# Block-sparse attention and gated MLP on one core: head 0's queries transposed in fp32, one mask product for two thirds, first attention products in slots 4 to 6

## The chip, the core and the metric

The kernel runs on one core of a Trainium2 chip. TensorE (PE) multiplies matrices into PSUM, VectorE (DVE), ScalarE (ACT) and GpSimd (POOL) do the elementwise work, and the queue of SyncE (SP) issues most of the DMAs; two DMAs are issued by ScalarE's queue. The metric is the time of one execution on the device in microseconds (us). A profiled execution gives the trace from which all lines here come: its instructions cover a span that is a little shorter than the execution's time.

## The reference

Inputs: `q`, `k`, `v` of shape (4, 8, 768, 64), fp32; three sampled key blocks for each of 24 query blocks; the weights of a gated MLP.

```python
scores = scale * np.matmul(q, k.transpose(0, 1, 3, 2))      # 4 x 8 heads, 768 x 768
mask = np.abs(blk_i - blk_j) <= 1                           # blocks of 32
mask = mask | (blk_i == 0) | (blk_j == 0) | (blk_i == 23) | (blk_j == 23)
# ... and for each query block its 3 sampled key blocks
attn = softmax(np.where(mask, scores, -1e9))
x = np.matmul(attn, v)  -> (4, 768, 512)
h = np.maximum(x @ w_in, 0.0); u, v = halves of h
v_s = einsum(w_spatial, layernorm(v)) + b_spatial
out = (u * v_s) @ w_out
```

The four batches need 32 heads of attention and four passes of the MLP.

## The kernel before, in words

**Data layout.** `kq` holds for each of 8 heads, on 128 partitions, the transposed keys (columns 0 to 767) and the transposed queries (columns 768 to 1535). Partitions 0 to 63 carry the head's 64 dimensions, partitions 64 to 127 the mask: one-hot block rows beside the keys, and for each query the penalty of each block beside the queries. One product of the two over 128 partitions is then score plus penalty, and the exponential makes masked entries zero. The mask rows are the same for all heads: they are made once for head 0 (`kq[MX, 0, ...]`, MX is partitions 64 to 127) and copied to the others by `rows`, partly on VectorE, partly on POOL, partly on ScalarE. The queries' mask rows are made by `mask_rows`: a product of `bm` (24 block rows) with the one-hot rows into PSUM, 256 columns (a third of the 768, TW) at a time, and a copy out of PSUM.

**Setup.** Keys and queries come as fp32 with 128 partitions of rows (`load`), are cast to bf16 (`cast`), transposed on TensorE against an identity (`head`, `tr`) and copied out of PSUM to `kq` (`split0` for pair 0, plain copies for the others). Pair 0 is heads 0 and 1, and head 0's parts come first: keys of chunks 0 to 3 on ScalarE's DMA queue, then queries of chunks 0 to 3 on the same queue, the rest on SP's. Head 0's keys are cast by ScalarE, its queries by POOL (`cast(0, "q", PL, H0, C03)`). In the cast the chunks are put in an order in which one transpose holds chunk i on its lower and chunk i + 2 on its upper 64 partitions, so `split0` copies chunks 0 and 1 from the lower half and 2 and 3 from the upper.

**Slots.** After the setup the work is dealt to slots, written out by hand. In slot s TensorE does the score products of one piece (`qk_unit`; from slot 36 on `qk_full`), into one of two PSUM buffers, and ScalarE takes their exponential. Since there are two buffers, the product of slot s waits for the exponential of slot s - 2. Units 0 and 1 are heads 0 and 1 of pair 0 with two thirds of the queries; each takes three slots. Slot 0 makes 4 small products in two PSUM tiles with an exponential for each; slot 2 makes the last two key chunks against 512 query columns. Behind the score product of a slot stand, on TensorE, in this order: what `pre` holds, the attention products (`av_unit`, three pieces of 8 products of 65 columns for a unit), what `at` holds, the MLP's steps (`run_queue`), what `late` holds. `av_at` says which attention piece stands in which slot: before, unit 0's three pieces stand in slots 5, 6 and 6.

Around the change: in slot 0 `second` transposes head 0's last two key chunks; in slot 1 `third` transposes head 1's keys and first queries (from POOL's casts of head 1); in slot 2 the third mask product follows; in slot 3 VectorE copies mask rows (`ROWS`); in slots 4, 7 and 9 the pairs 1, 2 and 3 are transposed (`tr_first`). POOL's stream after the setup is casts in the order of `ORDER`, as their loads land. Small products against `warm` (`filler`) keep TensorE at work in the setup: FILL at the start and FILL2 in three places.

**PSUM.** Four kinds of tile: two buffers "sc" for scores, two "av" for attention products, and "moeA" and "moeB", which `moe_tag` hands out in turn.

## Time and profile before

| | |
|---|---|
| median of 3 runs | 210.06 us (209.82 to 210.76) |
| profiled execution | 210.04 us |
| its span | 208.3 us |
| TensorE busy | 201.0 us (97%) |
| ScalarE busy | 168.4 us (81%) |
| VectorE busy | 146.8 us (70%) |
| POOL busy | 89.4 us (43%) |

A row of the timeline or of the chain gives the start and the length in us of one instruction or of several merged ones (x8), the engine, the line, the operation and the tiles as out<-in. In brackets stands the idle time of the engine ahead of it and what ended it. A row of the stage table gives a stretch, its length, then busy us and number of instructions for PE, PEld (the loading of weights), DVE, ACT and POOL, then the granted clock, the DMA engines' share and GB/s. Matmuls are pipelined: a length holds the way through the array, and the next one can start long before the end.

### The profile page before, as it was taken

How to read it: one execution, taken by the hardware profiler on the slowest of the kernel's cores; microseconds unless marked ns; L12 is line 12 of the kernel's file. 1: busy time of each engine (PE TensorE's matmuls, PEld its weight loads, DVE VectorE, ACT ScalarE, POOL GpSimd, SP SyncE). 2: the span in 40 equal slices, each digit the busy share in tenths (PEclk: the TensorE clock that was granted, in tenths of full speed). 3: DMA queues.
4: the chain of work that ended last, by engine and by line, in shares of the span. 5: the costliest groups of instructions: out<-in, count | busy, mean ns of one | idle time of the engine just before them, and what ended most of it. 6: DMA issues, size and time to landing. Idle time of an engine off the chain costs nothing.

```text
span 208.3 us, 5489 instructions
## 1 busy us (share of the span) xinstructions
PE 201.0 (97%) x2203; PEld 138.0 (66%) x2225; DVE 146.8 (70%) x315; ACT 168.4 (81%) x222; POOL 89.4 (43%) x186
## 2 busy tenths in 40 slices
PE   6899999999999999999999999999999999999993
PEld 6599888777766776667556676667665567445551
DVE  6888776989876766575975585456875666576871
ACT  6899999999999999989899878889899884266021
POOL 6888989767927964006757600006210000013000
PEclk9999999999999999999999999999999999999999
DMA  5999899999999999499987920499402010610016
GB/s 143 338 362 357 275 383 270 206 247 389 253 253 308 259 300 208 139 199 386 292 176 206 139 41 0 164 189 335 75 0 41 0 37 4 250 57 0 0 70 232
DMA packets 53053, 39.48 MB, mean 190 GB/s; under 512 B 33956, under 2 KB 47652, under 8 KB 53028
## 3 DMA queue, kind: packets, MB, share of 16 engines
q1 hardware_dynamic: 52596, 38.74, 70.0%
q10 hardware_dynamic: 432, 0.39, 0.6%
q8 instruction: 17, 0.28, 0.5%
q14 instruction: 8, 0.07, 0.1%
HBM read 24.77 MB, written 6.29 MB: 149 GB/s over the span
## 4 chain that ended last, share of the span: by engine, by line
PE 87%; DVE 4%; ACT 4%; DMA 2%; issue 1%; POOL 0%; ACTq 0%
PE ps L428 21%; PE ps_moe L630 17%; PE ps_moe L561 13%; PE ps_av L476 12%; PE ps L415 7%; PE ps_av L458 4%; PE ps_t L561 4%; PE ps_t L630 4%; PE ps_sc L630 2%; ACT a_all L420 2%; DVE stats L594 2%; DVE vn L185 2%; DMA st_q<-in_q_dram 2%; PE ps_sc L561 1%; PE ps L263 1%
## 5 line engine op out<-in xcount | busy, mean ns | idle before, releaser
L431 ACT ACTIVATE a_all<-ps 128x768 bf16<-128x768 f32 x144 | 113.4, 812 | 13.8 <-PE ps L428 6.2
L428 PE MATMUL ps<-kq 128*128 128x512 bf16 (+1 forms) x288 | 70.3, 326 | 0.3
L476 PEld LDWEIGHTS <-a_all 128*128 128x128 bf16 x864 | 46.6, 98 | 19.0
L476 PE MATMUL ps_av<-vv,a_all 128*128 128x65 bf16 x864 | 51.1, 194 | 0.1
L428 PEld LDWEIGHTS <-kq 128*128 128x128 bf16 x288 | 27.9, 97 | 23.6
L137 POOL CAST nat<-st_k 128x256 bf16<-128x256 f32 (+3 forms) x37 | 17.7, 509 | 38.7 <-DMA st_k<-in_k_dram 38.7
L420 ACT ACTIVATE a_all<-ps 128x1024 bf16<-128x1024 f32 x35 | 33.5, 1027 | 0.3
L630 PE MATMUL ps_moe<-w_spt,vn 128*128 128x512 bf16 (+1 forms) x144 | 33.1, 325 | 0.0
L598 POOL TENSOR_SCALAR std<-mv 128x3 f32<-128x3 f32 (+1 forms) x9 | 3.4, 376 | 48.7 <-DVE mv L595 48.5
L661 DVE TENSOR_TENSOR sb<-ps_moe,b_row 128x512 f32<-128x512 f32 x18 | 12.4, 690 | 14.5 <-PE ps_moe L630 14.2
L630 PE MATMUL ps_moe<-xt,w_in_t 128*128 128x256 bf16 (+1 forms) x108 | 21.7, 299 | 0.2
L415 PE MATMUL ps<-kq 128*128 128x256 bf16 x135 | 20.8, 275 | 0.8 <-DVE kq L211 0.6
L561 PE MATMUL ps_moe<-w_in_t,xt 128*128 128x512 bf16 x65 | 20.2, 378 | 0.2
L137 POOL CAST vv<-st_v 128x256 bf16<-128x256 f32 (+2 forms) x37 | 18.5, 533 | 3.9 <-DMA st_v<-in_v_dram 3.8
L137 POOL CAST nat<-st_q 128x256 bf16<-128x256 f32 (+2 forms) x41 | 19.2, 496 | 1.6 <-DMA st_q<-in_q_dram 1.5
L561 PE MATMUL ps_moe<-w_out_t,un 128*128 128x512 bf16 x64 | 19.4, 378 | 0.2
L441 DVE TENSOR_TENSOR xn<-ps_av,rc 128x384 bf16<-128x384 f32 (+1 forms) x36 | 18.5, 513 | 1.4 <-DVE rc L440 0.2
L664 DVE TENSOR_TENSOR un<-sb,un 128x512 bf16<-128x512 f32 x24 | 17.4, 727 | 1.5
L630 PEld LDWEIGHTS <-vn 128*128 128x128 bf16 x192 | 15.5, 97 | 4.4
L594 DVE BATCH_NORM_STATS2 stats<-vn 128x6 f32<-128x512 bf16 x24 | 16.5, 688 | 1.5 <-ACT vn L589 0.9
L211 DVE COPY osb<-ps_moe 128x512 f32<-128x512 f32 x12 | 8.3, 689 | 11.2 <-PE ps_moe L561 9.3
L211 DVE COPY kq<-tt 64x1536 bf16<-64x1536 bf16 x24 | 15.4, 641 | 0.6 <-DMA tt<-nat 0.2
(94 smaller groups left out, 241.6 us busy)
## 6 DMA issues: line engine op xcount, KB each, us to landing
out_dram<-osb SPq DMA_DIRECT2D x23, 256.0 KB, 2.1
st_k<-in_k_dram SPq DMA_DIRECT2D x15, 384.0 KB, 4.6
st_v<-in_v_dram SPq DMA_DIRECT2D x15, 384.0 KB, 6.2
st_q<-in_q_dram SPq DMA_DIRECT2D x12, 384.0 KB, 4.9
ws_f<-in_moe_w_spatial_dram SPq DMA_DIRECT2D x6, 384.0 KB, 5.5
w_f<-in_moe_w_in_dram SPq DMA_DIRECT2D x8, 256.0 KB, 6.3
w_f<-in_moe_w_out_dram SPq DMA_DIRECT2D x4, 256.0 KB, 5.4
st_q<-in_q_dram SPq DMA_DIRECT2D x3, 256.0 KB, 6.9
```

What stands on the lines that cost most here:

```text
L137: eng.tensor_copy(out=dst, in_=src)
L211: nc.vector.tensor_copy(out=o, in_=i)
L415: nc.tensor.matmul(out=ps[:, at:at + n * TW], lhsT=kq[:, h, ci * 128:(ci + 1) * 128], rhs=kq[:, h, qcols(t0, n)], start=True, stop=True)
L420: nc.scalar.activation(out=out, in_=ps, func=AF.Exp, scale=0.125)
L428: nc.tensor.matmul(out=ps[:, n0:n1], lhsT=kq[:, j % H, ci * 128:(ci + 1) * 128], rhs=kq[:, j % H, S + n0:S + n1], start=True, stop=True)
L431: nc.scalar.activation(out=a_ref["h", j][:, ci, :], in_=ps[:, 0:S], func=AF.Exp, scale=0.125)
L441: nc.vector.tensor_tensor(out=out, in0=ps[:, :, 0:D], in1=rc[:, 0:n].to_broadcast([128, n, D]), op=ALU.mult)
L476: nc.tensor.matmul(out=av_ref[j][:, qc, :], lhsT=a_ref["h", j][:, ci, qc * 128:(qc + 1) * 128], rhs=vv[p % NVV][:, h, ci, :], start=(ci == ...
L561: nc.tensor.matmul(out=ref["ps"][:, 0:w], lhsT=lhs(i), rhs=rhs(i), start=(i == 0), stop=(i == n - 1))
L594: nc.vector.bn_stats(out=stats, in_=self.vn[:, tcc, :])
L630: nc.tensor.matmul(out=o.rearrange("p (c t) -> p c t", c=n), lhsT=lhs(i)[:, (d0 + x) * 128:(d0 + x + 1) * 128], rhs=rhs(i), start=(i == 0) ...
L664: nc.vector.tensor_tensor(out=self.in_place(*area), in0=sb, in1=self.in_place(*area), op=ALU.mult)
```

## The change

1. `ident_f`, an fp32 copy of the identity, is made by POOL. A memset of part of `kq` goes, since no mask product reads it any more.
2. POOL's cast of head 0's queries goes. Four fp32 transposes read the loaded queries as they are: chunks 0 and 1, then 2 and 3, each once into `psq` and once into `psr`, two PSUM tiles of fp32. `q_part` copies 64x128 pieces: the lower halves from `psq` by VectorE, the upper halves from `psr` by ScalarE. The cast to bf16 happens in these copies.
3. One mask product over 512 columns (two thirds) takes the place of two over 256; it reads only the 24 mask partitions. Its copy out is on ScalarE, 512 wide.
4. Row copies of the keys' mask: head 2's goes whole to POOL (before: 512 columns on ScalarE and 256 on POOL), queued ahead of head 1's query cast. Head 5's moves from VectorE's setup to slot 3.
5. Fillers: 2 and 6 in place of 2, 2 and 2.
6. Unit 0's attention pieces stand in slots 4, 5 and 6. The one in slot 4 stands at the slot's end, after pair 1's transposes.

```diff
-    FILL, FILL2 = 26, (2, 2, 2)
+    FILL, FILL2 = 26, (2, 6)
...
+    ident_f = const.tile([128, 128], FP32)
...
-    nc.gpsimd.memset(kq[0:D, 1, 0:TW], 0.0)
+    nc.gpsimd.tensor_copy(out=ident_f, in_=ident)
...
-    cast(0, "q", PL, H0, C03)
     cast(0, "k", PL, H0, C45)
     cast(0, "k", PL, H1)
+    rows(slice(2, 3), K_, PL)
     cast(0, "q", PL, H1, C03)
...
-    def mask_rows(ps, t, copy, h=0, rs=slice(0, KR)):
-        nc.tensor.matmul(out=ps[:, 0:TW], lhsT=bm[rs], rhs=kq[rs, h, t * TW:(t + 1) * TW],
+    def mask_rows(ps, t, copy, h=0, rs=slice(0, KR), n=1):
+        nc.tensor.matmul(out=ps[:, 0:n * TW], lhsT=bm[rs], rhs=kq[rs, h, t * TW:(t + n) * TW],
                          start=True, stop=True)
-        copy(kq[MX, 0, qcols(t)], ps[0:MX.stop - MX.start, 0:TW])
+        copy(kq[MX, 0, qcols(t, n)], ps[0:MX.stop - MX.start, 0:n * TW])
...
     filler(FILL2[0], wps)
-    mask_rows(psum.tile([128, 1024], FP32, tag="sc", bufs=2, name="mq"), 0, act_copy, 1)
-    rows(slice(2, 3), slice(0, 512), nc.scalar)
+    mask_rows(psum.tile([128, 1024], FP32, tag="sc", bufs=2, name="mq"), 0, act_copy, 1, MR, 2)
+    psq = [psum.tile([128, 512], FP32, tag="av", bufs=2, name="psq"),
+           psum.tile([128, 512], FP32, tag=moe_tag(), bufs=1, name="psr")]
+    for i in range(TC):
+        for ps in psq:
+            nc.tensor.transpose(out=ps[:, i * 128:(i + 1) * 128],
+                                in_=st["q", 0][:, 0, 2 * i * D:2 * (i + 1) * D], identity=ident_f)
+
+    def q_part(i, odd, copy):
+        copy(kq[0:D, 0, S + (2 * i + odd) * 128:S + (2 * i + odd + 1) * 128],
+             psq[odd][odd * D:(odd + 1) * D, i * 128:(i + 1) * 128])
+
+    q_part(0, 0, dve_copy)
+    q_part(0, 1, act_copy)
+    split0(ps0, 0, *K4, 1)
     filler(FILL2[1], wps)
-    psq = bank("psq", "av")
-    head(psq, 0, *Q4)
-    split0(psq, 0, *Q4, 0)
-    split0(ps0, 0, *K4, 1)
-    filler(FILL2[2], wps)
-    mask_rows(psum.tile([128, 512], FP32, tag=moe_tag(), bufs=1, name="mq"), 1, act_copy, rs=MR)
-    split0(psq, 0, *Q4, 1)
-    rows(slice(4, 6), K_)
+    q_part(1, 0, dve_copy)
+    q_part(1, 1, act_copy)
+    rows(slice(4, 5), K_)
     rows(H1, qcols(0, 2), PL)
-    rows(slice(2, 3), slice(512, S), PL)
...
-    ROWS = [(3, 2, 8, qcols(0)), (5, 6, 8, K_),
+    ROWS = [(3, 2, 8, qcols(0)), (3, 5, 6, K_), (5, 6, 8, K_),
...
-            sl = (5, 6, 6)[e] if u == 0 else 3 * u + e + (4 if u < 3 else 3)
+            sl = (4, 5, 6)[e] if u == 0 else 3 * u + e + (4 if u < 3 else 3)
...
-        for u, e in av_at.get(s, []):
-            av_unit(u, e)
+        if s > 4:
+            for u, e in av_at.get(s, []):
+                av_unit(u, e)
...
         for f in late.get(s, []):
             f()
+        if s == 4:
+            av_unit(0, 0)
```

## The prediction

> **What bounds the kernel now.** I read the page's chain of waits first, to learn which engine carries the span, then the stage table, then the timeline of the first 14 us, which holds everything that the change touches.
>
> ```profile
> PE 87%; DVE 4%; ACT 4%; DMA 2%; issue 1%; POOL 0%; ACTq 0%
> ```
>
> TensorE carries the chain, so ScalarE's 81% on the page is not the bound over the whole run. The chain in order of time shows where TensorE takes over (start, length, what):
>
> ```profile
> 1.14 3.19 DMA st_q<-in_q_dram
> 4.39 0.57 POOL nat L137
> 6.11 1.09 ACT a_all L410 x2
> 7.19 3.77 ACT a_all L420 x4
> 11.01 0.60 PE ps L415 x4
> ```
>
> Up to 6.11 us one thread leads: head 0's queries land, POOL casts them, TensorE transposes them, VectorE copies them, the first product runs. Then ScalarE's exponentials lead until 11.01, and TensorE after that. The stage table confirms it (time, then TensorE's busy us out of 5):
>
> ```profile
> 5.00:10.00 5.00, 4.17 (x37) 2.84 (x39) 4.23 (x12) 4.45 (x8) 4.47 (x9) 1.00 1.01 330
> 10.00:15.00 5.00, 4.93 (x86) 4.38 (x83) 4.21 (x9) 4.98 (x7) 4.45 (x8) 1.00 1.08 363
> 15.00:20.00 5.00, 5.00 (x90) 4.68 (x88) 4.21 (x11) 5.00 (x6) 4.21 (x9) 1.00 1.09 375
> ```
>
> From 10 us on neither engine rests. TensorE's free time from 10 to 180 us, summed over all windows of that table, is 0.07 + 0.05 + 0.11 + 0.05 + 0.27 + 0.32 + 0.16 = 1.03 us. So a shift that reaches 11 us on both engines reaches the end, and nothing after it can add more than about a microsecond. The timeline of the setup:
>
> ```profile
> 4.29 0.38 ACT L214 ACTIVATE kq<-mq 64x256 bf16<-64x256 f32 x1
> 4.57 0.61 ACT L239 ACTIVATE kq<-kq 64x512 bf16<-64x512 bf16 x1
> 5.01 0.29 PE L276 MATMUL psq<-ident,nat 128*128 128x128 bf16 x2 [0.65 <-POOL nat L137]
> 5.34 0.28 DVE L211 COPY kq<-psq 64x256 bf16<-64x256 bf16 x1 [0.64 <-PE psq L276]
> 5.68 0.39 PE L407 MATMUL ps<-kq 128*128 128x256 bf16 x2
> 6.11 0.60 ACT L410 ACTIVATE a_all<-ps 128x512 bf16<-128x512 f32 x1
> 5.89 0.40 POOL L137 CAST nat<-st_q 128x256 bf16<-128x256 f32 x1 [0.24 <-DMA st_q<-in_q_dram]
> 6.35 0.86 POOL L241 COPY kq<-kq 64x512 bf16<-64x512 bf16 x1
> 7.16 0.40 POOL L241 COPY kq<-kq 64x256 bf16<-64x256 bf16 x1
> ```
>
> TensorE waits 0.65 us for POOL's cast, VectorE 0.64 us for the transposes. Those are what the change goes for. Call the exponential of slot n s(n). The rows give s(0) = 6.11, s(2) = 7.98, s(3) = 9.02, then 9.94, 10.84, 11.75, 12.65, s(8) = 13.72: a pitch of 0.905 where ScalarE is never kept waiting, 0.13 more before s(3) (product 3 waits for VectorE: 8.37 + 0.61) and 0.17 more before s(8) (product 8 starts at 13.09).
>
> **The change, part by part.**
>
> *First exponential.* The queries land at 1.14 + 3.19 = 4.33; POOL's cast started on them at 4.39, so the fp32 transposes start at 4.40. `ident_f` is long there: POOL's earlier work ends at 3.38, and a 128x128 cast (0.29, the first of the two k casts) takes the place of a 0.34 memset. No fp32 matmul is in this trace, so its price is bounded. Floor: the bf16 transpose, 0.056 (eight in 0.61, of which 0.22 is the length of one). Top: four times a weight load (0.097) and a matmul that don't overlap, 4 x 0.153 = 0.61. I take 0.153, one unhidden pair, because the instruction order shows these matmuls without a separate weight load, and the transpose only moves data. The Trainium skill ("TensorE: Matmul & The Clock Gate", Terms) says that trn2's transpose mode is 4x faster for FP32, which would also be one pass; by it the sum is the same, and no run here shows it.
>
> In the order of the changed kernel only the first copy on each engine carries a wait: VectorE's on the third transpose, ScalarE's on the fourth. Fourth result: 4.40 + 4 x 0.153 - 0.056 + 0.22 = 5.18. ScalarE starts at 5.21; a 64x128 copy is 0.27 by the rows for 256 columns (0.38) and 512 (0.60). It ends at 5.48, TensorE goes at 5.53 (before: 5.62 to 5.67), the exponential 0.44 later, as before: s(0) = 5.97, 0.14 early. Beside that path: ScalarE's mask copy, now 512 wide, runs 4.40 to 5.00 (mask product 3.97 + 0.39) and lets the next one in at 4.89; if the transposes came sooner it would be the limit. The six fillers end at 5.01 + 0.34 = 5.35, under the copy. ScalarE loses the 0.61 row copy and the second mask copy (0.38), which stood before s(0) with idle time around them, so nothing on the path. VectorE: first copy 5.05 to 5.34, `split0` to 5.65, second copy to 5.97, one head of rows instead of two (0.36 for 0.56): the second half of product 0 can go at 5.70, product 1 at 6.02, both before ScalarE asks.
>
> *POOL.* Without the query cast it takes k as it lands (4.14 and 4.70 by the issue times 1.23, 1.65 and 2.9, 3.1 us to landing): casts end at 5.26. The row copy that follows is 768 wide: 0.83 (a later POOL row of that size) to 1.26 (0.86 + 0.40). Head 1's query cast, queued behind it, ends at 6.61 to 7.04 instead of 6.29, and product 2 stands behind the transposes of that cast: s(2) not before 7.40 to 7.83. From s(0) it is 5.97 + 1.87 = 7.84. So this wait is just covered. POOL's next row copy ends by 7.96 at worst and VectorE's first head-1 query split at 7.93; product 3 goes at 8.0, is done at 8.61, before s(3) = 7.84 + 0.905 = 8.75. The old 0.13 stall is gone. POOL is free at 7.96, the next cast started at 7.79 (waiting for a DMA), so later casts slip by 0.2 at most; q1 is due at 9.35 on TensorE and was cast at 8.96. SP's order is the same; its k load that waits for POOL's k casts was issued at 6.65, after they end in both.
>
> *Attention products in slots 4 to 6.* Eight of 65 columns take 0.26 of issue. Product n starts 1.07 after s(n-2) at the earliest (10.04 to 10.09, 10.95 to 11.01). Slot 4: product 8.91 to 9.35, transposes (0.45) to 9.79, the moved eight to 10.05 (their v cast ended at 9.41). Product 5 could go at 9.82 and now goes at 10.05: done at 10.64, s(5) = 10.68 where 10.56 was due. That 0.12 is the price. Then product 6 at 10.74, eight more to 11.43, product 7 at 11.75 (after s(5)), transposes and the next eight to 12.89, product 8 at 12.89 against 13.09, s(8) = 13.54 against 13.72. Both engines are 0.19 early there.
>
> *VectorE in slot 3* gets 0.36 for head 5's rows after 0.82: free at 9.7, the transposed heads come at 9.87. Hidden by 0.15; past that product 6 (cover 0.11) slips with it.
>
> *After slot 8.* The tightest input is pair 3's query cast, 13.96, used at 14.48 and now at 14.29. The shift holds.
>
> Sum on the profiled execution (span 208.3, 210.04 with what lies around it, 0.02 under the median of 210.06): 210.04 - 0.19 = 209.85. In general the gain is 0.19 - (s(0) - 5.97), zero at a transpose of 0.20. At 0.056 s(0) is 5.65 by the mask copy and the gain is 0.2 to 0.5 by POOL's row copy: 209.5. A measurement of this kernel tells about 0.5%, 1.05 us, from no change.
>
> **The rivals.**
>
> 1. *Slower: fp32 costs four passes.* One mechanism at one place. With 0.61 each the fourth result is there at 4.40 + 2.44 - 0.056 + 0.22 = 7.00, s(0) = 7.79, 1.63 later than break-even: 211.7. It decides from 0.47 a transpose (1.05 us lost). For it: no row shows otherwise, and a 4-byte operand is twice bf16's. Against it: a transpose adds nothing up. The Trainium skill ("FP8 and Floating Point Precision", TensorE Precision Notes) gives true FP32 four passes through the array; by that page this rival would be the forecast, and no run here shows it yet.
> 2. *No gain or a small loss*: two passes (0.31) give s(0) = 6.60, a loss of 0.44, 210.5. Or the gain is there and VectorE's slot 3, or POOL's casts, take it back by slot 6: 210.0 to 210.3. For it: covers of 0.1 to 0.15 us, and 64-partition copies on POOL between 0.61 and 0.86 for one size.
> 3. *Faster by more than 1.05 us*: 0.5 from the setup and over half of the 1.03 us of TensorE's later gaps. Against it: those gaps hang on VectorE's statistics at 91 to 101 and 143 to 150 us, which move along. 208.9.
>
> **How the numbers follow.** Forecast, 209.5 to 210.05: 0.48. Rival 2, up to 211.1: 0.22. Rival 1: 0.22. Rival 3: 0.08. Faster 0.08, same 0.48 + 0.22 = 0.70, slower 0.22. The range goes from 209.2 (the floor of the transpose and a third of a microsecond of later gaps) to 211.8 (four passes, 211.7); the forecast's own is 209.5 to 210.05.
>
> **What would show it.** Right: the transposes at 4.40 ending near 5.0, first exponential near 5.97, no idle on ScalarE before s(3), 0.1 before s(5), product 8 near 12.9, and the same offset at 40 us. Wrong: an fp32 transpose over 0.2 us; TensorE waiting for head 1's query cast past 7.1; product 6 waiting for VectorE; or offsets that grow after 15 us, which would mean work that I took as hidden is not.

## The result, and the profile after

The changed kernel takes 210.92 us (median of 21 runs, 209.95 to 212.49), the kernel before 210.08 us (median of 21 runs, 209.74 to 210.76): a ratio of 1.0033, with an interval of 1.002 to 1.0045. It is slower by 0.7 us by the ratio and by 0.84 by the medians, where 0.19 us less was predicted. That is inside the 0.5% which the prediction counted as no change, but with 21 runs of each the interval leaves 1 out, and the sign is the other one. The new kernel also varies more: without its one run at 212.49 its runs cover 1.45 us, those of the kernel before 1.02 us, and the lowest runs of the two are only 0.21 us apart.

Its profiled execution took 210.71 us (span 208.9; before 210.04 and 208.3). The shares of its chain of waits, by engine, and the first of the longest pieces of that chain (start, length, what):

```profile
PE 94%; DVE 3%; ACT 1%; issue 0%; ACTq 0%
```

```profile
0.97 2.96 PE wps L180 x26
9.12 1.39 DVE kq L242 x2
10.55 0.68 DVE kq L212
11.26 0.69 DVE kq L212
11.99 1.05 DVE kq L242
```

The chain no longer runs through ScalarE's exponentials between 6 and 11 us. It goes through VectorE from 9.12 to 13.04, with two groups of row copies (line 242) in it, one of them 1.05 us long. The stage table:

```profile
5.00:10.00 5.00, 4.12 (x41) 2.98 (x41) 4.32 (x14) 4.67 (x9) 3.93 (x7) 1.00 1.01 342
10.00:15.00 5.00, 4.67 (x79) 3.97 (x77) 4.81 (x8) 4.88 (x6) 4.13 (x7) 1.00 1.09 362
15.00:20.00 5.00, 5.00 (x96) 4.70 (x93) 3.97 (x11) 4.89 (x6) 4.33 (x8) 1.00 1.06 369
```

From 10 to 15 us TensorE now rests 0.33 us (before: 0.07), while VectorE is busy for 4.81 instead of 4.21 us with one instruction fewer. So two places need an explanation: the start, and VectorE at 9 to 13 us. TensorE's timeline of the start:

```profile
3.72 0.42 PE L277 MATMUL ps<-ident,nat 128*128 128x128 bf16 x2
3.93 0.42 PE L180 MATMUL wps<-warm 128*128 128x128 bf16 x2
4.29 0.60 PE L270 MATMUL mq<-kq,bm 24*128 24x512 bf16 x1
4.82 0.33 PE L296 MATMUL psq<-ident_f,st_q 128*128 128x128 f32 x1
4.99 0.27 PE L296 MATMUL psr<-ident_f,st_q 128*128 128x128 f32 x1
5.10 0.27 PE L296 MATMUL psq<-ident_f,st_q 128*128 128x128 f32 x1
5.21 0.27 PE L296 MATMUL psr<-ident_f,st_q 128*128 128x128 f32 x1
5.86 0.38 PE L415 MATMUL ps<-kq 128*128 128x256 bf16 x2
```

The fp32 transposes follow each other by 0.11 us, which is less than the predicted 0.153. But they start at 4.82, not at 4.40, behind a mask product of 0.60 us. Up to there the bf16 matmuls of 128 columns start 0.107 us apart (two transposes from 3.72, the next matmul at 3.93); later in the same trace they start 0.056 us apart. In the trace of the kernel before the same step from 107 to 56 ns came at 3.69 us, here at 4.85 us. The page's clock row shows full speed from the first slice on in both kernels, because the trace's clock record only begins at the step: the pitch of equal matmuls tells it, the row doesn't. I call that time the change of pitch.

ScalarE follows:

```profile
4.92 0.59 ACT L215 ACTIVATE kq<-mq 64x512 bf16<-64x512 f32 x1 [0.63 <-PE mq L270]
5.54 0.44 ACT L215 ACTIVATE kq<-psr 64x128 bf16<-64x128 f32 x2
6.28 0.60 ACT L418 ACTIVATE a_all<-ps 128x512 bf16<-128x512 f32 x1 [0.30 <-PE ps L415]
```

Two ways lead from the mask product to ScalarE's first query copy at 5.54, and here they end almost together: the copy of the mask ends at 5.51, the fourth transpose at 5.48. So s(0), the start of the first exponential, is 6.28, later by 0.17 than the 6.11 of before. Against the kernel before, the exponentials are late by 0.17 at s(0), 0.04 at s(3), 0.17 at s(5), 0.14 at s(8), 0.42 at s(9), 0.58 at s(10) and 0.68 at s(20), and by 0.68 from there to the end. The larger part comes at s(9) and after. The rows of VectorE and of POOL there, in the changed kernel:

```profile
11.26 0.69 DVE L212 COPY kq<-ps 64x1024 bf16<-64x1024 bf16 x1
11.99 1.05 DVE L242 COPY kq<-kq 64x1536 bf16<-64x1536 bf16 x1
13.62 1.40 DVE L212 COPY kq<-ps 64x1024 bf16<-64x1024 bf16 x2
11.79 0.83 POOL L138 CAST vv<-st_v 128x768 bf16<-128x768 f32 x1 [0.25 <-DMA st_v<-in_v_dram]
```

The same instructions in the kernel before:

```profile
10.87 0.69 DVE L211 COPY kq<-ps 64x1024 bf16<-64x1024 bf16 x1
11.59 0.56 DVE L241 COPY kq<-kq 64x1536 bf16<-64x1536 bf16 x1
13.03 1.41 DVE L211 COPY kq<-ps 64x1024 bf16<-64x1024 bf16 x2 [0.21 <-PE ps L263]
11.66 1.19 POOL L137 CAST vv<-st_v 128x768 bf16<-128x768 f32 x1 [0.29 <-DMA st_v<-in_v_dram]
```

Before, VectorE's copy of the rows of heads 6 and 7 started 0.07 ahead of POOL's cast: the copy took 0.56 and the cast 1.19. Now the cast starts 0.20 ahead of the copy: the cast takes 0.83 and the copy 1.05. In these two traces whichever starts first keeps its own time, and the other pays. If the second stood still until the first had ended, the copy would end at 12.62 + 0.56 = 13.18 (measured 13.04) and the cast at 12.15 + 0.83 = 12.98 (measured 12.85), so this is within 0.14 us of a full block. The Trainium skill ("SBUF — State Buffer", Who interferes with whom) says that VectorE and GpSimd share a pair of ports, that in VectorE's two-port modes whoever issues first holds it for the whole instruction, and that issue order decides who blocks; the two traces agree with that order, and come within 0.14 us of that block.

The copy's extra half microsecond moves VectorE's next PSUM copies from 13.03 to 13.62, and product 9 waits for them:

```profile
13.66 0.42 PE L466 MATMUL ps_av<-vv,a_all 128*128 128x65 bf16 x8
14.35 0.61 PE L423 MATMUL ps<-kq 128*128 128x256 bf16 x4 [0.28 <-DVE kq L212]
```

### The profile page after: what moved, and what is told of

It is laid out like the page before. It is cut to its first block, busy times and chain, and to the rows that moved or that the text cites. A ratio compares the mean times of both kernels' runs of the same rounds, so it can differ in the third digit from the quotient of the medians.

```text
span 208.9 us, 5522 instructions
## 1 busy us (share of the span) xinstructions
PE 203.2 (97%) x2228; PEld 138.5 (66%) x2228; DVE 147.9 (71%) x316; ACT 168.3 (81%) x222; POOL 88.9 (43%) x185
## 4 chain that ended last, share of the span: by engine, by line
PE 94%; DVE 3%; ACT 1%; issue 0%; ACTq 0%
PE ps L436 22%; PE ps_moe L638 19%; PE ps_moe L569 15%; PE ps_av L484 13%; PE ps L423 6%; PE ps_t L569 4%; PE ps_av L466 4%; PE ps_t L638 4%; PE ps_sc L638 2%; DVE kq L212 2%; PE wps L180 2%; DVE kq L242 1%; PE ps_sc L569 1%; PE ps L264 1%; PE ps_av L264 1%; ACT kq L215 0%
## 5 line engine op out<-in xcount | busy, mean ns | idle before, releaser
L138 POOL CAST nat<-st_k 128x256 bf16<-128x256 f32 (+3 forms) x37 | 18.6, 532 | 41.4 <-DMA st_k<-in_k_dram 41.3
L606 POOL TENSOR_SCALAR std<-mv 128x3 f32<-128x3 f32 (+1 forms) x9 | 2.9, 317 | 48.1 <-DVE mv L603 48.0
L638 PE MATMUL ps_moe<-xt,w_in_t 128*128 128x256 bf16 (+1 forms) x112 | 22.9, 302 | 0.0
L569 PE MATMUL ps_moe<-w_in_t,xt 128*128 128x512 bf16 x72 | 22.3, 378 | 0.0
L423 PE MATMUL ps<-kq 128*128 128x256 bf16 (+1 forms) x136 | 21.0, 276 | 1.2 <-DVE kq L212 0.9
L569 PE MATMUL ps_moe<-w_out_t,un 128*128 128x512 bf16 x72 | 21.1, 378 | 0.0
L138 POOL CAST vv<-st_v 128x256 bf16<-128x256 f32 (+2 forms) x37 | 17.6, 508 | 3.8 <-DMA st_v<-in_v_dram 3.8
L138 POOL CAST nat<-st_q 128x256 bf16<-128x256 f32 (+2 forms) x40 | 18.3, 485 | 0.9 <-DMA st_q<-in_q_dram 0.9
L672 DVE TENSOR_TENSOR un<-sb,un 128x512 bf16<-128x512 f32 x24 | 16.7, 695 | 1.5
```

Source lines behind the costliest of these rows:

```text
L138: eng.tensor_copy(out=dst, in_=src)
L423: nc.tensor.matmul(out=ps[:, at:at + n * TW], lhsT=kq[:, h, ci * 128:(ci + 1) * 128], rhs=kq[:, h, qcols(t0, n)], start=True, stop=True)
L569: nc.tensor.matmul(out=ref["ps"][:, 0:w], lhsT=lhs(i), rhs=rhs(i), start=(i == 0), stop=(i == n - 1))
L638: nc.tensor.matmul(out=o.rearrange("p (c t) -> p c t", c=n), lhsT=lhs(i)[:, (d0 + x) * 128:(d0 + x + 1) * 128], rhs=rhs(i), start=(i == 0) ...
L672: nc.vector.tensor_tensor(out=self.in_place(*area), in0=sb, in1=self.in_place(*area), op=ALU.mult)
```

## The experiments

Five theories went into the runs. **A:** VectorE's new row copy in slot 3 (head 5) starts the delay. **B:** the new setup is exposed to the slow pitch, which lasts for a different time in each execution. **C:** the attention products in slot 4. **D:** VectorE's row copies collide with POOL's casts. **E:** the mask product over 24 partitions instead of 88 makes TensorE pause before and after it. Ratios are to the kernel before, run on the same chip beside them (its median there was 209.99 to 210.2). "Late" is the start of an exponential against the profile of before.

| kernel | median us | ratio, interval | change of pitch, us | s(0) | late at s(40) |
|---|---|---|---|---|---|
| changed, first profile | 210.92 | 1.0033, 1.002 to 1.0045 | 4.85 | 6.28 | 0.68 |
| e1, changed, head 5's rows on POOL | 210.85 | 1.003, 1.0018 to 1.0041 | 5.15 | 6.39 | 0.80 |
| e2, changed, attention in 5, 6, 6 | 210.5 | 1.0009, 0.9996 to 1.0022 | 5.46 | 6.54 | 0.57 |
| e3, before, head 5's rows in slot 3 | 210.02 | 0.9992, 0.9982 to 1.0001 | 4.94 | 5.98 | 0.04 |
| e4, before, attention in 4, 5, 6 | 210.25 | 1.0004, 0.9991 to 1.0016 | 6.86 | 6.11 | 0.30 |
| e5, changed, mask product over 88 | 210.2 | 1.0016, 0.9999 to 1.0033 | 3.93 | 5.94 | -0.21 |
| e8, before, with the new setup alone | 210.65 | 1.0027, 1.0012 to 1.0042 | 4.14 | 6.02 | 0.01 |
| e9, changed, rows of 6 and 7 in slot 8 | 210.39 | 1.0021, 1.0008 to 1.0034 | 6.80 | 7.01 | 0.85 |
| e10, before, rows of 6 and 7 in slot 8 | 209.94 | 0.9997, 0.9985 to 1.0009 | 5.86 | 6.06 | 0.31 |
| e6, changed, 2 warm-up matmuls | 211.86 | 1.0085, 1.0068 to 1.0101 | 10.25 | 6.86 | 2.20 |
| e7, before, 2 warm-up matmuls | 210.81 | 1.0036, 1.0024 to 1.0047 | 7.17 | 6.14 | 0.50 |
| e11, changed, mask product in two | 211.15 | 1.0048, 1.0034 to 1.0061 | 4.59 | 6.86 | 1.13 |
| e12, changed, transposes first | 210.54 | 1.0019, 1.0008 to 1.0031 | 4.86 | 6.42 | 0.62 |
| e13, e12 with a copy on VectorE | 210.31 | 1.0008, 0.9996 to 1.0019 | 5.72 | 6.22 | 0.38 |
| e14, e13, rows of 6 and 7 in slot 8 | 210.53 | 1.0016, 1.0007 to 1.0025 | 5.13 | 6.38 | 0.26 |

The last three columns are of one execution, the medians of 4 to 21.

### Is it VectorE's row of head 5, or the attention products?

e1, on the changed kernel:

```diff
+    rows(slice(5, 6), K_, PL)
...
-    ROWS = [(3, 2, 8, qcols(0)), (3, 5, 6, K_), (5, 6, 8, K_),
+    ROWS = [(3, 2, 8, qcols(0)), (5, 6, 8, K_),
```

> The changed kernel, but head 5's mask rows are copied by POOL in the setup, right after head 1's, and not by VectorE in slot 3. Theory A (VectorE): the changed kernel's loss arises in slots 3 to 9, because VectorE's copy of head 5's rows runs while POOL is in a cast and takes 0.66 us instead of 0.36, and pushes the copies of pair 2 so that product 9 waits. Then here pair 2's first copy starts near 13.2 instead of 13.62, the exponential of slot 9 comes about 0.4 us sooner relative to slot 0's, and the time falls by 0.3 to 0.45 us against the changed kernel, to 210.4 to 210.6. Theory B (setup): the loss is the first exponential, late because the weights and matmuls of the setup still run at the slow clock; then nothing moves behind slot 0 and the time stays at 210.8 to 211.0. Theory C (attention product in slot 4): the stall of 0.12 us ahead of slot 5 carries on; no change either.

Theory A falls for this loss: the time stays at 210.85, and VectorE's rows of heads 6 and 7 still run from 11.88 to 12.97, beside POOL's cast.

e2, on the changed kernel (e4 is the reverse edit on the kernel before):

```diff
-            sl = (4, 5, 6)[e] if u == 0 else 3 * u + e + (4 if u < 3 else 3)
+            sl = (5, 6, 6)[e] if u == 0 else 3 * u + e + (4 if u < 3 else 3)
...
-        if s == 4:
-            av_unit(0, 0)
```

> The changed kernel with unit 0's attention pieces back in slots 5, 6 and 6. Theory C: the 0.12 us stall ahead of the exponential of slot 5 goes, and the time falls by about 0.1 us. Theory A: slot 5 comes 0.12 us sooner but product 9 still waits for VectorE, so the end doesn't move (within 0.1 us of the changed kernel). Theory B: no change.

> The kernel before with one edit: unit 0's attention pieces in slots 4, 5 and 6. Theory C: the exponential of slot 5 comes about 0.1 us late and stays late, 210.2. Theories A and B: what TensorE does earlier in slot 4 it no longer has to do in slot 6, so the end stays within 0.1 us of 210.08.

The stall before s(5) is the attention products': s(5) comes 0.90 after s(4) in e2 and 1.04 after it in the changed kernel. But e2's s(3) comes 1.17 after s(2), where the changed kernel has 0.91; the wait only moves. e2's ratio is lower by 0.0024 (0.5 us) all the same, and its trace has no step at s(9). VectorE's copies of rows 6 and 7 take 1.00 us there too, and the PSUM copies behind them end at 15.02 as in the changed kernel; but the exponentials were already 0.56 late at s(3), so nobody waits for them. A late start hides the collision: the two losses don't add. On the kernel before the slot is worth nothing that can be measured (e4). So C is a term of the size the prediction gave it. It isn't the cause alone, since e8 below has the attention pieces in 5, 6 and 6 as well and loses 0.57 us. But e2 gives back more than any other single edit of the changed kernel, and why it gives back that much isn't shown: its interval and e8's overlap.

e3, on the kernel before:

```diff
-    rows(slice(4, 6), K_)
+    rows(slice(4, 5), K_)
...
-    ROWS = [(3, 2, 8, qcols(0)), (5, 6, 8, K_),
+    ROWS = [(3, 2, 8, qcols(0)), (3, 5, 6, K_), (5, 6, 8, K_),
```

> The kernel before with one edit: head 5's mask rows are copied by VectorE in slot 3, not in the setup. Theory A: VectorE gets a copy of 0.36 to 0.66 us between its slot 3 copy and pair 1's copies, product 9 comes 0.2 to 0.45 us later, and the time rises to 210.3 to 210.5; slots 0 to 3 stay or come 0.1 us sooner. Theories B and C: no change, 210.08.

No loss: there the copies of rows 6 and 7 still start first (11.48 against POOL's 11.65) and take 0.56. Head 5's row, which runs beside a cast, takes 0.66 instead of 0.36 even here.

### Is it the collision?

e9 on the changed kernel (e10 is the same edit on the kernel before):

```diff
-    ROWS = [(3, 2, 8, qcols(0)), (3, 5, 6, K_), (5, 6, 8, K_),
+    ROWS = [(3, 2, 8, qcols(0)), (3, 5, 6, K_), (8, 6, 8, K_),
```

> The changed kernel with one edit: VectorE's key row copy of heads 6 and 7 stands in slot 8 instead of slot 5. Theory D (collision): in the kernel before, this copy starts at 11.59, just ahead of POOL's v cast at 11.66, and takes 0.56 us while POOL's takes 1.19; in the changed kernel it comes second (11.99 against 11.80), ends 0.41 us after POOL's cast and takes 1.05, and pair 2's copies and with them product 9 wait for it. With the copy out of the way pair 2's first copy starts near 13.2 to 13.3, the exponential of slot 9 follows that of slot 8 by 0.92 to 1.0 us instead of 1.20, and the time falls by 0.3 to 0.45 us against the changed kernel, 210.5 to 210.6. Theory B (setup): the loss sits ahead of slot 0; the time stays at 210.8 to 210.95.

> The kernel before with the same edit. Theory D: VectorE's copy is ahead of POOL's cast there, so nothing is to be won: within 0.15 us of the kernel before; POOL's v cast takes 0.83 us instead of 1.19. If the copy in slot 5 loses the race in some executions of the kernel before as well, the time falls by 0.1 to 0.2 us. Theory B: no change.

In e9 the step at s(9) is gone: s(9) comes 0.92 after s(8), as in the kernel before, and all that is lost (0.86) is there before s(8): 0.90 at s(0), 0.77 at s(3), 0.90 again at s(5). The ratio falls from 1.0033 to 1.0021, 0.25 us, less than its interval is wide. In e10's one profile 0.39 us is lost between s(11) and s(20), over half of it at s(12), ahead of which the moved copy of 64x1536 runs beside a POOL cast and takes 1.09; the time is unchanged.

### Is it the setup?

e8 has the setup of the changed kernel and everything else of the kernel before:

```diff
-    rows(slice(4, 5), K_)
+    rows(slice(4, 6), K_)
...
-    ROWS = [(3, 2, 8, qcols(0)), (3, 5, 6, K_), (5, 6, 8, K_),
+    ROWS = [(3, 2, 8, qcols(0)), (5, 6, 8, K_),
...
-            sl = (4, 5, 6)[e] if u == 0 else 3 * u + e + (4 if u < 3 else 3)
+            sl = (5, 6, 6)[e] if u == 0 else 3 * u + e + (4 if u < 3 else 3)
```

> The setup of the changed kernel alone: fp32 transposes, one mask product, head 2's rows on POOL, the fillers; head 5's rows stay in VectorE's setup and the attention pieces in slots 5, 6 and 6 as before. Theory B: the first exponential is late by 0.1 to 0.5 us, the more the later TensorE's matmuls go over from 107 to 56 ns, and the time is 210.6 to 210.9. Theory C (attention pieces): the setup costs nothing on the whole, 210.1 to 210.3, as the kernel with the attention pieces put back came out at 1.0009. Theory D: 0.2 to 0.4 us lost where VectorE's copy of heads 6 and 7 comes after POOL's v cast has begun, nothing where it comes first.

The setup alone loses 0.66 us by the medians (0.57 by the ratio), although its profiled execution (210.05, change of pitch at 4.14, s(0) at 6.02) is level with the kernel before. One profile can't stand for the median here: its other runs reach 211.33.

e5 makes the mask product read 88 partitions, the lower 64 of them zeroed, as the kernel before did:

```diff
+    nc.gpsimd.memset(kq[0:D, 1, 0:2 * TW], 0.0)
...
-    mask_rows(psum.tile([128, 1024], FP32, tag="sc", bufs=2, name="mq"), 0, act_copy, 1, MR, 2)
+    mask_rows(psum.tile([128, 1024], FP32, tag="sc", bufs=2, name="mq"), 0, act_copy, 1, slice(0, KR), 2)
```

> The changed kernel with the mask product over 88 partitions (the lower 64 of them zeros, as in the kernel before) instead of the 24 mask partitions. Theory E (drain): TensorE doesn't overlap the 24-partition product with its neighbours: it starts 0.25 us after the filler ahead of it and the transposes 0.53 us after it. With 88 partitions it starts 0.11 us after the filler and the transposes 0.43 us later (0.22 at the fast clock), so the fourth transpose and the first exponential come 0.2 to 0.25 us sooner at the same change of clock. Against it: the waits are those of VectorE's mask, and nothing moves. In the time: 0 to 0.2 us less than the changed kernel, by theory D little, since product 9 waits for VectorE at 14.3 either way.

Its profiled execution, with an early change of pitch, comes out at the predicted numbers:

```profile
3.93 0.28 PE L181 MATMUL wps<-warm 128*128 128x128 bf16 x2
4.16 0.39 PE L271 MATMUL mq<-kq,bm 88*128 88x512 bf16 x1
4.39 0.27 PE L297 MATMUL psq<-ident_f,st_q 128*128 128x128 f32 x1
4.72 0.27 PE L297 MATMUL psr<-ident_f,st_q 128*128 128x128 f32 x1
4.59 0.59 ACT L216 ACTIVATE kq<-mq 64x512 bf16<-64x512 f32 x1 [0.29 <-PE mq L271]
5.20 0.44 ACT L216 ACTIVATE kq<-psr 64x128 bf16<-64x128 f32 x2
```

The mask product takes 0.39 instead of 0.60, the transposes start at 4.39, s(0) is 5.94, and the shift is -0.16 at s(0) and -0.20 from s(8) to the end: 209.86 us. It gets there by another path than the predicted one: the fourth transpose is done at 4.99, and the query copy starts at 5.20, when ScalarE's copy of the mask has ended. The median of its 12 runs is 210.2 all the same, and the highest 211.3.

This trace can't tell E from B: its mask product starts 0.17 after the last small matmul where the changed kernel's starts 0.25 after it, but the pitch differs too. The second trace of the kernel before (e17, below) can, since it has both kinds at the slow pitch. Its first mask product, over 88 partitions, starts 0.107 us after the matmul ahead of it, and the next matmul 0.213 after it; for its second, over 24, these are 0.246 and 0.322 (e11 has 0.247 and 0.320). So E is real: at the slow pitch the 24 partitions hold TensorE for a quarter of a microsecond more. But the kernel before has such a product too, and its two mask products together hold TensorE longer than the changed kernel's one (0.89 against 0.78 us, the pause ahead included), so E doesn't set the two kernels apart.

e6 and e7 make the slow pitch last longer: 2 small matmuls instead of 26 at the front of each kernel.

```diff
-    FILL, FILL2 = 26, (2, 6)
+    FILL, FILL2 = 2, (2, 6)
```

> The changed kernel with 2 small warm-up matmuls at the front instead of 26, so that TensorE is idle early and its matmuls of 128 columns keep the 107 ns pitch through the setup. Theory B (the setup's 512-wide mask product and fp32 transposes are exposed to the slow pitch; first exponential later by 0.37 us for each us by which the pitch changes later): the pitch still 107 ns when head 0's transposes run, s(0) at 6.8 to 7.3 against 6.28 in the changed kernel's profile, and the time 0.4 us or more above the changed kernel's 210.9. Theory D (the loss is mainly the collision of VectorE's row copies with POOL's casts): s(0) may move, but the loss stays under 0.3 us against the changed kernel.

> The kernel before with 2 small warm-up matmuls at the front instead of 26. Theory B: its setup waits for POOL's cast of the queries and so hides the slow pitch until about 6 us: s(0) at 6.0 to 6.3 as before, later exponentials up to 0.4 us late, the time at most 0.4 us above its own 210.0, so the gap to the changed kernel under the same edit grows from 0.8 to 1.0 us or more. If instead both kernels lose alike, the slow pitch is not what sets them apart.

TensorE in the changed kernel (e6):

```profile
4.11 0.60 PE L270 MATMUL mq<-kq,bm 24*128 24x512 bf16 x1
4.64 0.47 PE L296 MATMUL psq<-ident_f,st_q 128*128 128x128 f32 x1
4.91 0.42 PE L296 MATMUL psr<-ident_f,st_q 128*128 128x128 f32 x1
5.12 0.42 PE L296 MATMUL psq<-ident_f,st_q 128*128 128x128 f32 x1
5.34 0.42 PE L296 MATMUL psr<-ident_f,st_q 128*128 128x128 f32 x1
6.19 0.64 PE L415 MATMUL ps<-kq 128*128 128x256 bf16 x2
```

and in the kernel before (e7):

```profile
4.61 0.42 PE L276 MATMUL psq<-ident,nat 128*128 128x128 bf16 x2
5.50 0.61 PE L407 MATMUL ps<-kq 128*128 128x256 bf16 x2
```

At the slow pitch an fp32 transpose takes 0.213 us. The changed kernel's first product starts 0.69 later than that of before; s(0) is 6.86 against 6.14. Its loss against the uncut kernel before is 1.76 us, that of before 0.71. This is what B asked for, though the kernel before loses more than the 0.4 us that was expected: with the same slow pitch in the setup the old setup keeps its s(0) and the new one doesn't. Not all of the 1.05 us between them is the setup, though: the pitch changed at 10.25 in e6's profile and at 7.17 in e7's, so e6's products of slots 1 and 2 were slow as well (late by 1.17 at s(1) and 1.65 at s(2), against 0.36 and 0.37).

### Taking both away

e11 cuts the mask product in two, the second behind the fillers:

```diff
+    nc.tensor.matmul(out=mq[:, 0:TW], lhsT=bm[MR], rhs=kq[MR, 1, 0:TW], start=True, stop=True)
...
     filler(FILL2[1], wps)
+    mq1 = psum.tile([128, 512], FP32, tag="av", bufs=2, name="mq")
+    nc.tensor.matmul(out=mq1[:, 0:TW], lhsT=bm[MR], rhs=kq[MR, 1, TW:2 * TW], start=True, stop=True)
```

> The changed kernel with its 512-wide mask product cut in two of 256 columns: the first where the whole one stood, the second behind the six fillers into an attention tile; two ScalarE copies of 256 columns. Theory B: at the same time of the change of pitch s(0) comes about 0.2 us sooner than in the changed kernel while the pitch is slow (0.25 us less of the product ahead of the transposes), the same when it is fast; time 210.5 to 210.8. Theory D: unchanged, 210.8 to 211.0.

It missed for a reason of its own:

```profile
6.14 0.28 PE L310 MATMUL mq<-kq,bm 24*128 24x256 bf16 x1 [0.54 <-DVE kq L212]
```

The second half waits 0.54 for VectorE's query copies, which suggests that its PSUM buffer is the one they read, and s(0) is 6.86. It says nothing about B.

e12 puts the transposes ahead of both mask products, drops the fillers between them, and has the attention products in 5, 6, 6; e13 gives the second mask copy to VectorE; e14 also has the rows of heads 6 and 7 in slot 8.

```diff
-    filler(FILL2[0], wps)
-    mask_rows(psum.tile([128, 1024], FP32, tag="sc", bufs=2, name="mq"), 0, act_copy, 1, MR, 2)
...
                                 in_=st["q", 0][:, 0, 2 * i * D:2 * (i + 1) * D], identity=ident_f)
...
     q_part(0, 0, dve_copy)
+    nc.tensor.matmul(out=mq[:, 0:TW], lhsT=bm[0:KR], rhs=kq[0:KR, 1, 0:TW], start=True, stop=True)
     q_part(0, 1, act_copy)
+    act_copy(kq[MX, 0, qcols(0)], mq[0:MX.stop - MX.start, 0:TW])
...
+    filler(4, wps)
+    nc.tensor.matmul(out=mq1[:, 0:TW], lhsT=bm[0:KR], rhs=kq[0:KR, 1, TW:2 * TW], start=True, stop=True)
     q_part(1, 0, dve_copy)
     q_part(1, 1, act_copy)
+    act_copy(kq[MX, 0, qcols(1)], mq1[0:MX.stop - MX.start, 0:TW])
```

e13, on e12:

```diff
-    act_copy(kq[MX, 0, qcols(1)], mq1[0:MX.stop - MX.start, 0:TW])
+    dve_copy(kq[MX, 0, qcols(1)], mq1[0:MX.stop - MX.start, 0:TW])
```

> The changed kernel with the transposes of head 0's queries ahead of the mask products, no fillers between, two 256-wide mask products over 88 partitions (lower 64 zero), the second behind four fillers, and the first attention pieces in slots 5, 6, 6 again. Theory B: with nothing slow ahead of them the four fp32 transposes start at 4.0 to 4.3, s(0) is at 5.7 to 6.0 whether the pitch is slow or fast, and the time is 209.7 to 210.0, level with the kernel before or 0.3 us under it. Theory D: product 9 still waits for VectorE's rows of heads 6 and 7, s(9) minus s(8) is 1.1 to 1.2 instead of 0.92, and the time stays 210.3 or more.

> The kernel with the transposes ahead of both mask products, and the copy of the second mask product on VectorE instead of ScalarE, where it had stood between the last query copy (ending at 6.00) and the first exponential (6.42). Theory B (slow pitch and copies ahead of the first exponential): s(0) at 6.0 to 6.1 with the slow pitch and 5.7 to 5.9 with the fast one, in the mean under the 6.11 of the kernel before; if theory D holds too, product 9 still waits for VectorE's rows of heads 6 and 7, and the time is 210.0 to 210.4. If B were all, 209.8 to 210.0.

> The same with the key rows of heads 6 and 7 in slot 8 instead of 5, so that neither named cause is left. B and D together: s(9) minus s(8) at 0.92, the shift constant from there on, and the time 209.7 to 210.1, level with or under the kernel before and 0.2 to 0.4 under the same kernel with those rows in slot 5. If it stays at 210.4 or more, a third cause is missing.

In e12 the transposes start right behind the key transposes, at 3.93, so the queries were there by then:

```profile
3.72 0.42 PE L278 MATMUL ps<-ident,nat 128*128 128x128 bf16 x2
3.93 0.42 PE L295 MATMUL psq<-ident_f,st_q 128*128 128x128 f32 x1
4.57 0.42 PE L295 MATMUL psr<-ident_f,st_q 128*128 128x128 f32 x1
```

But four of them at 0.213 each hold TensorE until 4.79, and ScalarE's four copies in a row (the last, of the mask, from 6.02 to 6.40) then set s(0) at 6.42, where 5.7 to 6.0 was expected. Its step at s(9) is there, as D said (s(9) comes 1.17 after s(8)). e13, without that last copy on ScalarE, has s(0) at 6.22, and its time, 210.31, can't be told from that of the kernel before, although VectorE's rows of heads 6 and 7 took 1.14 in its trace. e14 missed: with no step at s(9) it stays at 210.53, and by its own expectation a third cause is missing then. In its trace the transposes started at 4.12, s(0) was 6.38, 0.28 late, and 0.26 of that is left at the end. Its interval overlaps that of e13, so this pair doesn't give the size of D, and none of these kernels beats the kernel before.

### The same kernels once more

Two more traces of the changed kernel and one more of the kernel before, to see what differs between executions:

> The changed kernel as it is, for a second trace of it. In the first one 0.17 of the 0.67 us of loss was there at s(0), and 0.54 came at products 9, 10 and 20, where VectorE's row copies ran beside POOL's casts. Theory B: s(0) follows the time at which the matmul pitch changes, 6.28 + 0.37 x (that time - 4.85) within 0.15 us. Theory D: the steps at s(9), s(10) and s(20) come again, 0.4 us or more in sum; if they are absent here, the collision depends on which engine starts first in that execution.

> The changed kernel once more, for a third trace. The same two expectations as for the second: s(0) on the line 6.28 + 0.37 x (time of the change of pitch - 4.85) within 0.15 us, and, by theory D, 0.4 us or more in the steps at s(9), s(10) and s(20).

> The kernel before as it is, for a second trace of it. Theory B: s(0) within 0.1 us of 6.11 whatever the time at which the pitch changes, and if that is later than 5 us, s(3) 0.1 to 0.4 us late. Theory D: VectorE's rows of heads 6 and 7 start ahead of POOL's v cast and take 0.56, no step at s(9) or s(10).

| trace | time, us | change of pitch | s(0) | late at s(0) | at s(8) | at s(40) |
|---|---|---|---|---|---|---|
| changed, first | 210.71 | 4.85 | 6.28 | 0.17 | 0.14 | 0.68 |
| changed, second (e15) | 210.78 | 6.38 | 6.80 | 0.69 | 0.74 | 0.73 |
| changed, third (e16) | 210.48 | 4.67 | 6.23 | 0.12 | 0.32 | 0.40 |
| before, first | 210.04 | 3.69 | 6.11 | 0 | 0 | 0 |
| before, second (e17) | 210.19 | 6.42 | 6.11 | 0.00 | 0.13 | 0.11 |

In the second trace nearly all of the loss is there at s(0). TensorE in it:

```profile
4.29 0.60 PE L270 MATMUL mq<-kq,bm 24*128 24x512 bf16 x1
4.82 0.47 PE L296 MATMUL psq<-ident_f,st_q 128*128 128x128 f32 x1
5.51 0.42 PE L296 MATMUL psr<-ident_f,st_q 128*128 128x128 f32 x1
5.73 0.81 PE L180 MATMUL wps<-warm 128*128 128x128 bf16 x6
6.37 0.39 PE L415 MATMUL ps<-kq 128*128 128x256 bf16 x2
```

The four transposes cover 4.82 to 5.93 (5.48 in the first trace), the six fillers, meant to fill a gap, run at the slow pitch up to 6.37, and the first product starts right behind them, 0.51 later than in the first trace. The kernel before had its change of pitch just as late in its second trace, and s(0) at 6.11 again. What B expected there, a setup that waits for POOL's cast of the queries and hides the slow pitch, isn't what its trace shows:

```profile
3.78 0.40 POOL L137 CAST nat<-st_q 128x256 bf16<-128x256 f32 x1 [0.40 <-DMA st_q<-in_q_dram]
4.57 0.42 PE L276 MATMUL psq<-ident,nat 128*128 128x128 bf16 x2
5.46 0.61 PE L407 MATMUL ps<-kq 128*128 128x256 bf16 x2
```

The queries landed earlier than in the first trace, where the cast starts at 4.39, and TensorE goes through its setup without waiting for them. From the small matmul at 4.04 to the first product the old setup takes 1.42 us (to 5.46), the new one 2.33 (to 6.37). Four fp32 transposes in place of two in bf16 are 0.69 of the difference, two more fillers 0.21. The kernel before pays for the slow pitch later, with 0.13 at s(3). Its rows of heads 6 and 7 start ahead of POOL's cast (11.60 against 11.97) and take 0.56, as D expected.

The third trace is mostly D, at another place than the first. VectorE and POOL in it:

```profile
9.80 1.00 DVE L242 COPY kq<-kq 64x768 bf16<-64x768 bf16 x1
10.83 0.68 DVE L212 COPY kq<-ps 64x1024 bf16<-64x1024 bf16 x1
9.76 0.83 POOL L138 CAST nat<-st_k 128x768 bf16<-128x768 f32 x1 [0.30 <-DMA st_k<-in_k_dram]
```

POOL's cast starts 0.04 ahead of head 5's row copy, which takes 1.00 instead of 0.36 us. Product 6 then waits 0.4 for VectorE's copies, s(6) comes 1.25 after s(5) instead of 0.905, and it is 0.47 late. The rows of heads 6 and 7 start first this time (12.27 against 12.29) and take 0.56. So the row that theory A named can cost time, though the loss comes without it too (e1).

For B, s(0) of the traces with the changed setup follows the change of pitch: 3.93 and 5.94 (e5), 4.14 and 6.02 (e8), 4.67 and 6.23, 4.85 and 6.28, 5.15 and 6.39 (e1), 5.46 and 6.54 (e2), 6.38 and 6.80, 6.80 and 7.01 (e9). From first to last this is 1.07 us of s(0) for 2.87 us, 0.37 for each. With the old setup s(0) stays between 5.98 and 6.11 over changes from 3.69 to 6.86.

The executions without a kept trace can be sorted too. Each has a mean granted clock on record, and in the 17 traced executions with the full warm-up it rounds to less than 1.000 exactly when the change came at 5.72 us or later. By that sign the changed kernel has a median of 211.16 us in its 8 late executions and of 210.69 in the other 13; the setup alone (e8) 210.98 in 5 and 210.41 in 7; e5 211.15 in 3 and 210.14 in 9; the kernel before 210.26 in 50 and 209.97 in 52. So a late change goes with 0.5 to 1.0 us in these three kernels with the new setup and 0.3 in the old one, which bears B out. It isn't all: e8's 7 early executions are 0.63 above the early ones of the kernel before beside them (209.78), which neither the line for s(0) nor any trace explains.

## Why the prediction was wrong

**The step that failed: "so the fp32 transposes start at 4.40", and with it s(0) = 5.97.** The working took the landing of the queries as the last thing that TensorE waits for, and a mask product of "3.97 + 0.39" ahead of them. The queries were no limit (e12 uses them at 3.93). The mask product started at 4.29, took 0.60 and ended at 4.89; the transposes started at 4.82 behind it, and ScalarE's copy of the mask, put at 4.40 to 5.00 beside the path, ran from 4.92 to 5.51. The query copy that waits for both started at 5.54 instead of 5.21. The durations had been read from an execution in which the pitch happened to change at 3.69 us, before the setup's work. In the other executions of kernels with the full warm-up the change fell anywhere from 3.93 to 6.86. The Trainium skill ("TensorE: Matmul & The Clock Gate", What's actually happening) has a window of 3413 ns that runs freely and doesn't start with the kernel; the observed times, which span 3.17 us, agree with that, while the ±500 ns that the same section of the Trainium skill gives for the transition is much less than they show. Where the change is early the predicted numbers come out (e5: 4.39, 5.94 and -0.20), but by luck: the transposes were cheaper than priced (done at 4.99 instead of 5.18), and the mask copy, which was to let the next copy in 0.49 after its own start, let it in after 0.61 and became the limit. In the median of the executions they don't come out.

**Why the new setup pays more.** The prediction counted TensorE's and VectorE's waits of 0.65 and 0.64 us for POOL's cast as time to be won. They belong to the execution that was profiled. Of the six traces with the old setup two have that cast start at 4.39 and 4.42 (before, e3) and four at 3.59 to 3.81 (e4, e7, e10, e17), and in these four TensorE doesn't wait for it. There the change has no wait to win, and puts 0.91 us more of TensorE's work ahead of the first product at the slow pitch. That s(0) is 6.11 in both traces of the kernel before is a coincidence of two paths: a late cast at the fast pitch, an early one at the slow pitch. The slow pitch was in none of the three rivals; that 210.92 lies in the band that the prediction gave rival 2 (up to 211.1) owes nothing to this mechanism.

**The price of an fp32 transpose.** Taken at 0.153, bounded by 0.056 and 0.61. Measured 0.108 to 0.110 at the fast pitch and 0.213 at the slow one, twice the bf16 transpose's 0.056 and 0.107 each time. The trace has a weight load for each of them, of 0.14 us, which the prediction thought absent; it overlaps the transpose ahead. Rival 1, four passes, falls. Rival 2's two passes fit the ratio, but not its price of 0.31. The Trainium skill's four passes for true FP32 ("FP8 and Floating Point Precision", TensorE Precision Notes), which the prediction named, don't describe these transposes; no fp32 product was run. The slow pitch was not among the bounds, so an execution with 0.213 lies above the 0.20 at which the prediction had the gain end.

**"Hidden by 0.15; past that product 6 (cover 0.11) slips with it."** Right as a condition, and its row was mis-sized: 0.36 was read where nothing ran beside it. It took 0.66 in the first trace and 1.00 in the third, where product 6 slipped and s(6) lost 0.35.

**"The shift holds" after slot 8.** Wrong in the first trace: it looked for late inputs and not for copies that grow. VectorE's rows of heads 6 and 7 took 1.05 for 0.56 and product 9 waited. In the kernel before they were first by 0.07 us, so it took no more than a small shift between VectorE and POOL to turn it round. Rival 2 had this place ("VectorE's slot 3, or POOL's casts, take it back") and the variation on POOL (0.61 to 0.86 for one size), at a price of up to 0.45 instead of what it brought; it didn't have the mechanism.

**Right.** The old stall of 0.13 before s(3) is absent in the first trace (s(3) comes 0.91 after s(2)), though not in the second and third (1.11 and 1.03). The attention products in slot 4 cost 0.13 before s(5) where s(3) had not stalled (0.12 predicted), and nothing where it had. Product 8 started at 13.22, where 12.89 plus the actual delay of s(0), 0.31, gives 13.20. A shift that is there at 25 us reaches the end unchanged.

**What the sum now looks like.** First trace: 0.17 at s(0), -0.03 up to s(8), 0.54 from collisions after it (0.28 and 0.16 at s(9) and s(10), 0.10 by s(20)). Second: 0.69 at s(0), 0.04 after it, no collision that counts. Third: 0.12, then 0.35 at s(6), -0.17 recovered by s(8), 0.10 at s(10). Both causes are shown: the start carries 0.69 of the 0.73 us of the second trace, collisions 0.54 of the 0.68 of the first. Where the start is late enough, as in e2, it covers the collision, so there the loss is nearer to the larger of the two than to their sum. How they divide in the median stays open: by the ratios, putting the attention products back alone (e2) gave back 0.5 us, taking the collision at slot 5 away (e9) 0.25, changing the setup and the slot of the attention products (e13) 0.5, and all of it together (e14) 0.36, and the intervals of these runs reach over 0.2 us to each side. So e13 doesn't show that repairing the setup gives back anything beyond the attention slots. After e14 a third cause is not ruled out; the mask product's 24 partitions (E) are not it, since e14 uses 88.

## What to carry to other kernels

Before a wait is taken out of a kernel's first microseconds, look at several executions, since one profile shows one moment of the change of pitch and one landing of the inputs: the wait may not be there in the others. Price the instructions that take its place on the path at the slow pitch too. Where VectorE copies from SBUF to SBUF while POOL casts, a row's length from the trace holds only for the order of starts in that trace; note who was first and by how much, and count a margin under 0.2 us as none.

## What the runs showed of the hardware that was not expected

- The change from 107 to 56 ns between 128-column matmuls came at 3.69 to 6.86 us from the span's start in kernels with the same 26 warm-up matmuls, at 7.17 and 10.25 with 2.
- An fp32 transpose of 128 by 128 costs 0.108 us at the fast pitch and 0.213 at the slow one.
- At the slow pitch a product of 256 columns over 24 partitions, between matmuls over 128, took 0.25 us more of TensorE's time than one over 88 (both in e17).
- The first queries, whose DMA is issued at 1.14 or 1.15 us in each of the six traces with the old setup, were cast from 3.59 us on in one of them and from 4.42 on in another.
- A VectorE copy of 64x768 in bf16 that started 0.04 us after a POOL cast took 1.00 instead of 0.36 us, one of 64x1536 that started 0.20 after one took 1.05 instead of 0.56; a POOL cast that started 0.07 after such a copy took 1.19 instead of 0.83.
